# Pairs of tokens in 512-byte packets for the opening's queries and keys, with the third unit's values on all rows and several loads moved

## The chip, the cores and the metric

The kernel runs on one core of a Trainium2 chip. The metric is the device time of one execution in microseconds (us), as the median of several runs. The engines are TensorE (PE; PEld is its weight load), VectorE (DVE), ScalarE (ACT), GpSimd (POOL) and SyncE (SP), which issues most of the DMAs.

## The reference

Three stages follow one another: chunked attention with memory tokens, an MLP with a leaky ReLU, and an MLP with a rational function, all in float32.

```python
# attention: B, H, S, D = 4, 8, 768, 64; chunks of 32 queries
k_ctx = k[:, :, l_start:r_end]          # 16 tokens left, 8 right of the chunk
k_full = np.concatenate([mem_k, k_ctx], axis=2)     # 8 memory tokens ahead
v_full = np.concatenate([mem_v, v_ctx], axis=2)
scores = scale * np.matmul(q_c, k_full.transpose(0, 1, 3, 2))
a = np.exp(scores - np.max(scores, axis=-1, keepdims=True))
a = a / (np.sum(a, axis=-1, keepdims=True) + 1e-09)
out[:, :, c_start:c_end] = np.matmul(a, v_full)
# first MLP: 3072 tokens, 512 -> 2048 -> 512
h = x @ w_in;  x = np.maximum(0.01 * h, h) @ w_out
# second MLP, the same sizes
h = x @ w_in;  P = a0 + a1*h + a2*h**2 + a3*h**3
Q = 1 + abs(b0)*abs(h) + abs(b1)*h**2
out = (P / (Q + 1e-6)) @ w_out
```

The weights arrive as float64 and are read as pairs of 32-bit words.

## The kernel before, in words

The 3072 tokens are cut into six tiles of 512. Each MLP goes over its tiles, and in each over 16 columns of 128 hidden features: `emit_h` makes a column (`hps`), `leaky` or `rational` its activation, `emit_y` or `emit_o` adds its share to four accumulators (`acc`). A float32 product is made of three: each operand is split into a rounded part and a rest (`xh`, `xl`; `wh`, `wl`). A weight pair (`pair_load`, `pair_scale` on ScalarE, `pair_join` on VectorE, `pair_hi` on ScalarE, `pair_lo` on VectorE) holds one column of `w_in` and one of `w_out`, which is why the first tile of the first MLP also prepares all weights.

Attention comes in three forms. The **opening** makes the first 512 tokens before any MLP work, as four units of 128 tokens: `unit_k` and `unit_q` (transposes on TensorE, then copies into `okT` and `oqT`), `unit_b` (a copy into a ring on GpSimd), `unit_s` (scores of a unit), `unit_m` (maximum and subtraction, VectorE), `unit_e` (exponential, ScalarE), `unit_n` (sum and division), `unit_t` (transposes of the weights, copies into `pT`), `unit_x` (product with the values), `side_h` and `side_l` (split into `xh` and `xl`). Then `emit_first` makes the first columns of `hps` (L841). The **narrow** form (`att_*`) makes the second tile beside the first tile's MLP, 64 tokens at a time, and the **wide** form (`wide_*`) the others, 128 at a time, turning q and k through DRAM (`turn_out`, `turn_in` with the `park` tensors).

What sets the order: the opening is written out by hand under a manual schedule, in which each engine takes its instructions in the order of the code. In the main loop, `narrow_plan` and `wide_plan` put their steps into numbered slots, two for each column. All loads but a few are issued by SP in the order of the code. In the opening the loads of q and k are eight DMAs of 128 tokens with one token and head per packet (256 bytes), L978 and L986; then come the values (`room_v`, 16 DMAs, L320) and the weights (L167). After the opening's code come the loads of the weight pairs 2 to 4, of the narrow queries and keys, of the narrow values for blocks 8 and 9 (`load_v`, with their memory rows L344), and the coefficients (L1075, L1076). The next pair's load, the sixth, is issued in the main loop by `pairs_ahead`.

Units 0 and 1 have their weights for the product with the values on all 128 rows (two halves of 64 context rows, zero where they don't belong, written by two copies of 64 rows each); units 2 and 3 keep one copy of 128 rows and take twice as many products of 32 columns on 64 rows.

Of the kernel before, what the change touches and what calls it, by code (L numbers as in the profile page):

```python
# [16 lines left out]
P = 128  # L17
QB = 64
# [6 lines left out]
def kernel(  # L25
# [92 lines left out]
    pmore = wpool.tile([P, 2 * H * QB], F32, tag="w", name="pmore")  # L118
# [274 lines left out]
    pT = [t.rearrange("p n e c m k -> p (n e c) m k") for t in (pall, pall2)]  # L393
    pT += [pmore[:, u * H * QB:(u + 1) * H * QB] for u in range(2)]
    kraw = [early[0][:, u * H * D:(u + 1) * H * D] for u in range(U)]
    qraw = [early[1][:, u * H * D:(u + 1) * H * D] for u in range(U)]
# [15 lines left out]
    def turn(t, rows, ps):  # L412
        for c in range(NP):
            nc.tensor.transpose(ps[:, c * rows:(c + 1) * rows], t[:rows, c * P:(c + 1) * P], ident[:rows, :rows])
        return ps[:, :NP * rows].rearrange("p (c m) -> p c m", c=NP)
# [4 lines left out]
    def unit_small():  # L420
        pv = turn(sraw, NS, psa.tile([P, 512], F32, tag="acc", name="pso"))
# [4 lines left out]
        def border(u, i):  # L426
            for half in range(2):
                nc.vector.tensor_copy(out=okT[half][:, :, TAT + u * P:TAT + u * P + RCTX],
                                      in_=pv[:, half * HP:(half + 1) * HP, NM + i * RCTX:NM + (i + 1) * RCTX])

        border(1, 0)
        return lambda: border(U, 1)

    def unit_k(u, engs):
        pv = turn(kraw[u], P, psw.tile([P, 512], F32, tag="ps", name="psk"))
        at = TAT + u * P
        lo = RCTX if u == 1 else 0
        for half, eng in enumerate(engs):
            copy_on(eng, okT[half][:, :, at + lo:at + P], pv[:, half * HP:(half + 1) * HP, lo:])

    def unit_b(u, eng):
        n = P // CHUNK
        to, at = u * n % RING, RING + u * n
        for half in range(2):
            eng.tensor_copy(out=okB[half][:, :, to:to + n, NM:], in_=okB[half][:, :, at:at + n, NM:])

    def unit_q(u):
        pv = turn(qraw[u], P, psw.tile([P, 512], F32, tag="ps", name="psq"))
        nc.scalar.mul(out=oqT[:, :, u * P:(u + 1) * P], in_=pv, mul=scale)
# [3 lines left out]
    def unit_s(u):  # L453
        ps = psw.tile([P, 512], F32, tag="ps", name="pss").rearrange("p (c b m) -> p c b m", b=2, c=NP)
        for b in range(2):
            at = (2 * u + b) * QB
            for p in range(NP):
                for e in range(2):
                    r = slice(e * 64, e * 64 + 64)
                    for c in range(2):  # L460
# [4 lines left out]
                                         okB[p // HP][r, p % HP, lo:hi + 1:hi - lo, :], start=True, stop=True)  # L465
        ops[u] = ps
# [24 lines left out]
    def unit_t(u):  # L491
# [9 lines left out]
        if u >= 2:  # L501
# [5 lines left out]
    def unit_x(u):  # L507
        if u < 2:
            oxv[u] = psa.tile([P, 512], F32, tag="acc", name="psx")
# [7 lines left out]
        if u == 2:  # L517
            oxv[2] = [psw.tile([P, 512], F32, tag="ps", name="psx").rearrange("p (c u m) -> p c u m", c=NP, u=2)
                      for b in range(2)]
        pt = pT[u].rearrange("p (c e h m) -> p c e h m", c=NP, e=2, h=2)  # L520
        order = [(c, p, b) for p in range(NP) for c in range(2) for b in range(2)]
        if u == U - 1:
            order.sort(key=lambda x: (x[0], x[0] * x[2]))
        for c, p, b in order:
            r = slice(b * SB, b * SB + SB)
            for e in range(2):
# [716 lines left out]
```

## Time and profile before

| | us |
|---|---|
| median of three runs (1139.67 to 1139.99) | 1139.88 |
| the profiled execution | 1139.51 |
| its span, first to last instruction | 1137.7 |
| TensorE busy | 1127.1 |
| first `hps` matmul starts | 27.41 |

Granted TensorE clock 1.00 in all slices of the profile, full speed. All times in the rows below count from the start of the span, so a difference found in them is a difference of the execution. Busy times of TensorE overlap a little, since matmuls are pipelined; what matters is when a group starts and whether an idle time, in brackets, stands behind it.

### The profile page before, as it was taken

What the parts mean: (1) busy time and instruction counts of PE and PEld (TensorE: products, weight loads), DVE (VectorE), ACT (ScalarE), POOL (GpSimd) and SP (SyncE); (2) the same over time, 40 slices, a digit from 0 to 9 for tenths busy, and PEclk for the clock granted to TensorE, in tenths of its full rate; (3) what the DMA queues carried; (4) which work ended last, traced back from release to release, by engine and by line L of the source; (5) the groups of instructions that cost most, each with busy time, mean ns of one, the idle gap of its engine ahead of it and who ended that gap; (6) DMA issues with size and microseconds to landing.
All of it is one profiled execution on the core that took longest, in us unless ns stands there. A gap on an engine that the chain in (4) does not pass through costs nothing.

```text
span 1137.7 us, 19657 instructions
## 1 busy us (share of the span) xinstructions
PE 1127.1 (99%) x7626; PEld 922.3 (81%) x7626; DVE 766.0 (67%) x1315; ACT 628.5 (55%) x1138; POOL 237.4 (21%) x274
## 2 busy tenths in 40 slices
PE   8999999999999999999999999999999999999998
PEld 6777788888888888888888888888888888888887
DVE  5888754555645555542346886887887887788775
ACT  5687422232232223223347777776776777777765
POOL 5000302132211332210000222221222222222222
PEclk9999999999999999999999999999999999999999
DMA  9876777797778778732343002001001100100000
GB/s 208 240 223 201 192 228 209 202 257 200 209 210 237 195 203 238 215 114 94 93 138 119 21 1 74 1 1 62 13 1 37 39 1 17 58 1 3 35 1 37
DMA packets 146921, 131.59 MB, mean 116 GB/s; under 512 B 61744, under 2 KB 117392, under 8 KB 146828
## 3 DMA queue, kind: packets, MB, share of 16 engines
q1 hardware_dynamic: 141604, 122.80, 38.0%
q0 software_dynamic: 4864, 7.45, 2.8%
q8 instruction: 60, 0.98, 0.4%
q14 instruction: 33, 0.27, 0.1%
q10 hardware_dynamic: 360, 0.08, 0.0%
HBM read 92.52 MB, written 37.75 MB: 115 GB/s over the span
## 4 chain that ended last, share of the span: by engine, by line
PE 94%; SPq 2%; DMA 2%; DVE 1%; ACT 1%; issue 0%; DVEq 0%; ACTq 0%
PE hps L853 44%; PE acc L949 23%; PE acc L911 22%; PE psx L754 2%; SPq L320 1%; PE pss L712 1%; DMA wr<-in_moe_w_out_dram 1%; DMA early<-in_v_dram 0%; SPq L344 0%; SPq L167 0%; DMA early<-in_q_dram 0%; PE psx L601 0%; PE pss L554 0%; DMA pb<-park_dram 0%; PE hps L841 0%
## 5 line engine op out<-in xcount | busy, mean ns | idle before, releaser
L911 PE MATMUL acc<-g,w 128*128 128x512 f32 x1152 | 278.3, 391 | 0.0
L949 PE MATMUL acc<-w,g 128*128 128x512 f32 x1152 | 275.5, 389 | 0.0
L949 PEld LDWEIGHTS acc<-w,g 128*128 128x128 f32 x1152 | 216.3, 188 | 44.8
L911 PEld LDWEIGHTS acc<-g,w 128*128 128x128 f32 x1152 | 214.9, 188 | 45.0
L889 POOL TENSOR_TENSOR g<-R,g 128x512 fp32r<-128x512 f32 x96 | 124.4, 1296 | 504.4 <-ACT g L888 449.6
L863 ACT ACTIVATE g<-hps 128x512 fp32r<-128x512 f32 x96 | 57.4, 598 | 300.7 <-PE hps L853 300.7
L853 PE MATMUL hps<-xh,w 128*128 128x512 f32 x752 | 205.2, 396 | 0.4 <-DVE w L195 0.4
L853 PE MATMUL hps<-yh,w 128*128 128x512 f32 x768 | 204.1, 389 | 0.0
L866 DVE TENSOR_TENSOR g<-s,g 128x512 fp32r<-128x512 f32 x96 | 66.3, 690 | 179.8 <-ACT s L864 176.6
L853 PEld LDWEIGHTS hps<-yh,w 128*128 128x128 f32 x768 | 144.2, 188 | 29.9
L853 PEld LDWEIGHTS hps<-xh,w 128*128 128x128 f32 x752 | 138.5, 188 | 30.1 <-DVE w L195 0.8
L677 POOL DMA_DIRECT2D vb<-in_v_dram x128 | 83.2, 651 | 262.6 <-PE psx L754 211.5
L876 ACT ACTIVATE A<-hps 128x512 f32<-128x512 f32 x96 | 57.1, 595 | 113.9 <-PE hps L853 113.8
L892 DVE SCALAR_TENSOR_TENSOR A<-A,small,pb 128x512 f32<-128x512 f32 x96 | 72.0, 750 | 55.9 <-ACT pb L877 55.8
L853 PE MATMUL hps<-yl,w 128*128 128x512 f32 x384 | 102.7, 389 | 0.0
L853 PE MATMUL hps<-xl,w 128*128 128x512 f32 x376 | 100.9, 390 | 0.0
L883 DVE SCALAR_TENSOR_TENSOR A<-A,pb 128x512 f32<-128x512 f32 x96 | 66.8, 695 | 30.1 <-ACT pb L896 30.1
L853 PEld LDWEIGHTS hps<-yl,w 128*128 128x128 f32 x384 | 72.1, 188 | 14.9
L853 PEld LDWEIGHTS hps<-xl,w 128*128 128x128 f32 x376 | 70.6, 188 | 15.3
L878 ACT ACTIVATE R<-hps,small 128x512 f32<-128x512 f32 x96 | 75.0, 781 | 0.0
L885 DVE SCALAR_TENSOR_TENSOR R<-R,small,A 128x512 f32<-128x512 f32 x96 | 72.2, 752 | 3.4
L894 DVE SCALAR_TENSOR_TENSOR R<-R,small,hps 128x512 f32<-128x512 f32 x96 | 71.8, 748 | 3.4
(126 smaller groups left out, 1136.7 us busy)
## 6 DMA issues: line engine op xcount, KB each, us to landing
wr<-in_moe_w_in_dram SPq DMA_DIRECT2D x32, 512.0 KB
wr<-in_moe_w_out_dram SPq DMA_DIRECT2D x32, 512.0 KB
park_dram<-pb SPq DMA_DIRECT2D x16, 512.0 KB
pb<-park_dram SPq DMA_DIRECT2D x64, 128.0 KB
w_dram<-wwall SPq DMA_DIRECT2D x32, 256.0 KB
wb<-w_dram SPq DMA_DIRECT2D x32, 256.0 KB
kb<-in_k_dram SPq DMA_DIRECT2D x59, 112.0 KB
vb<-in_v_dram POOLq DMA_DIRECT2D x118, 56.0 KB, 3.5
```

Of the source, the lines that this page charges most:

```text
L677: nc.gpsimd.dma_start(out=vw[r + at:r + at + n, c], in_=v[bi, hs, lo:lo + n, :].rearrange("h p d -> p h d"))
L853: nc.tensor.matmul(ps[:, :n], w_[:, ws], x_[:, kk, :], start=(kk == 0 and m == 0), stop=(kk == KC - 1 and m == 2))
L863: nc.scalar.activation(out=gh, in_=ps, func=AF.Prelu, alpha=0.01)
L866: return [lambda: nc.vector.tensor_tensor(out=gl, in0=s, in1=gh.bitcast(F32), op=ALU.subtract)]
L878: nc.scalar.activation(out=R, in_=ps, func=AF.Identity, scale=ncf[:, 3:4], bias=ncf[:, 2:3])
L883: nc.vector.scalar_tensor_tensor(out=A0, in0=A0, scalar=ONE, in1=U0, op0=ALU.add, op1=ALU.mult)
L885: nc.vector.scalar_tensor_tensor(out=R0, in0=R0, scalar=ncf[:, 0:1], in1=A0, op0=ALU.add, op1=ALU.mult)
L889: nc.gpsimd.tensor_tensor(out=gl, in0=R0, in1=gh.bitcast(F32), op=ALU.subtract)
L892: nc.vector.scalar_tensor_tensor(out=A, in0=A, scalar=babs[:, 1:2], in1=U, op0=ALU.mult, op1=ALU.add)
L894: nc.vector.scalar_tensor_tensor(out=R, in0=R, scalar=ncf[:, 1:2], in1=ps, op0=ALU.add, op1=ALU.mult)
L911: nc.tensor.matmul(acc[i][d][:, :n], w_[:, ws], g_, start=(f == 0 and m == 0), stop=(f == FC - 1 and m == 2))
L949: nc.tensor.matmul(acc[i][s], g_[:, ss], w_, start=(f == 0 and m == 0), stop=(f == FC - 1 and m == 2))
```

## The change

1. The opening's q and k are loaded as groups of 256 tokens: partition p holds tokens 2p and 2p+1 of each head, which lie together in DRAM, so a packet has 512 bytes. The first group comes in two halves of four heads each (L995 on of the new file), the second whole: six DMAs instead of eight.
2. A transposed tile then holds the two tokens of a pair in its upper and lower 64 rows. `pairs_out` parts them by four copies of 64 rows by 256 columns for each half of the heads, with a step of two in the output. The first group's and the second queries' copies alternate between ScalarE and VectorE (`mix`); the second keys' are on ScalarE.
3. Scores and ring copies are made by halves of the heads, and the order of the units is new. Unit 2 now has its weights on all 128 rows, as units 0 and 1.
4. Unit 3's multiplication by the reciprocal sum goes from VectorE to GpSimd, and one cast of its output from ScalarE to VectorE.
5. The values of blocks 8 and 9 are loaded in the main loop, behind the weight pair of that column; the coefficients are loaded and scaled near the end of the first MLP. The first wide block's loads come three slots earlier, its queries' transposes and their reading back two.

The diff, cut to its core:

```diff
@@ views
-    pT += [pmore[:, u * H * QB:(u + 1) * H * QB] for u in range(2)]
-    kraw = [early[0][:, u * H * D:(u + 1) * H * D] for u in range(U)]
+    pT = [t.rearrange("p n e c m k -> p (n e c) m k") for t in (pall, pall2, pall)] + [pmore]
+    kraw, qraw = ([early[n][:, g * 2 * H * D:(g + 1) * 2 * H * D].rearrange("p (h m) -> p h m", h=H)
+                   for g in range(G)] for n in range(2))
@@ helpers
+    def pairs_of(src, g, hs):
+        return src[0, hs, g * 2 * P:(g + 1) * 2 * P, :].rearrange("h (p t) d -> p h (t d)", t=2)
+
+    def turn_pairs(t, half, ps):
+        for i in range(H // 2):
+            nc.tensor.transpose(ps[:, i * P:(i + 1) * P], t[:, half * (H // 2) + i], ident)
+
+    def pairs_out(ps, o, to, lo, engs, op):
+        for e in range(2):
+            for t in range(2):
+                i = ps[t * 64:t * 64 + 64].rearrange("p (c e m) -> p c e m", c=HP, e=2)[:, :, e, lo:]
+                op(engs[2 * e + t], o[e * 64:e * 64 + 64, :, to + 2 * lo + t:to + 2 * P:2], i)
...
+    def pairs_k(g, half, engs):
+        p, tag = (psa, "acc") if g else (psw, "ps")
+        ps = p.tile([P, 512], F32, tag=tag, name="psk")
+        turn_pairs(kraw[g], half, ps)
+        pairs_out(ps, okT[half], TAT + g * 2 * P, RCTX // 2 if g else 0, engs, copy_on)
...
+    def pairs_q(g, half, engs):
+        ps = psw.tile([P, 512], F32, tag="ps", name="psq")
+        turn_pairs(qraw[g], half, ps)
+        pairs_out(ps, oqT[:, half * HP:(half + 1) * HP], g * 2 * P, 0, engs, scale_on)
@@ wide_plan
-        put(at[n0] - 7, lambda: wide_load_qk(n0))
-        put(at[n0] - 6, lambda: wide_q(n0))
-        put(at[n0] - 5, lambda: turn_in(0, n0, wqT[n0]), lambda: wide_k(n0))
+        put(at[n0] - 10, lambda: wide_load_qk(n0))
+        put(at[n0] - 8, lambda: wide_q(n0))
+        put(at[n0] - 6, lambda: turn_in(0, n0, wqT[n0]))
+        put(at[n0] - 5, lambda: wide_k(n0))
@@ first loads
+        load_pairs(kraw, k, 0, LOWER)
...
+        load_pairs(qraw, q, 0, LOWER)
+        load_pairs(kraw, k, 0, UPPER)
+        load_pairs(qraw, q, 0, UPPER)
...
+        load_pairs(kraw, k, 1)
+        load_pairs(qraw, q, 1)
@@ the opening (new order)
+        mix = (act, dve, act, dve)
+        pairs_k(0, 0, mix)
+        unit_small()
+        unit_b(0, 0, pool)
+        unit_b(1, 0, pool)
+        pairs_q(0, 0, mix)
+        pairs_k(0, 1, mix)
...
+        unit_s(0, 0)
+        unit_s(1, 0)
+        pairs_q(0, 1, mix)
+        unit_s(0, 1)
+        unit_s(1, 1)
+        unit_m(0)
+        unit_m(1)
...
+        pairs_k(1, 0, (act,) * 4)
+        unit_e(0)
+        pairs_k(1, 1, (act,) * 4)
+        unit_e(1)
+        unit_n(0, pool)
+        pairs_q(1, 0, mix)
+        pairs_q(1, 1, mix)
...
+        unit_s(3, 1)
+        unit_m(2)
+        spread = unit_t(0)
+        unit_m(3)
+        run(spread)
+        unit_e(2)
...
+        unit_x(2)
...
+        side_h(2)
+        side_l(1)
+        unit_x(3)
+        warm(3)
+        side_h(3, 0)
+        side_h(3, 1, dve)
         emit_first(0, (0, 2))
-        load_v(FIRST)
-        load_v(FIRST + 1)
-        nc.sync.dma_start(out=coef[:, 0:4], in_=a.partition_broadcast(P))
-        nc.sync.dma_start(out=coef[:, 4:6], in_=b.partition_broadcast(P))
@@ main loop
-                if c == FC:
+                if c == NA - FC + 2:
+                    nc.sync.dma_start(out=coef[:, 0:4], in_=a.partition_broadcast(P))
+                    nc.sync.dma_start(out=coef[:, 4:6], in_=b.partition_broadcast(P))
+                if c == NA - 5:
                     nc.scalar.mul(out=ncf, in_=coef[:, 0:4], mul=-1.0)
...
                 pairs_ahead()
+                if c < 3:
+                    load_v(FIRST + c - 1)
```

The order of instructions at three places follows. On **ScalarE, in the opening**, around the four exponentials (`psk` and `psq` are transposed keys and queries, `pm` the scores on their way to weights, `pst` transposed weights, `psx` products). Before:

```order
L480 ACTIVATE pm<-pm 128x512
L418 COPY early<-psk 128x2x128 x2
L449 ACTIVATE early<-psq 128x4x128
L418 COPY early<-psk 128x2x128 x2
L449 ACTIVATE early<-psq 128x4x128
L480 ACTIVATE pm_104<-pm_104 128x512
L499 COPY pb<-pst 64x16x32 x2
L480 ACTIVATE pm_104<-pm_104 128x512
L538 CAST xh<-psx 128x4x128
L480 ACTIVATE pm_105<-pm_105 128x512
```

Now:

```order
L428 COPY early<-psk 64x2x124 x4
L496 ACTIVATE pm<-pm 128x512
L428 COPY early<-psk 64x2x124 x4
L496 ACTIVATE pm_104<-pm_104 128x512
L452 ACTIVATE early<-psq 64x2x128 x4
L515 COPY pb<-pst 64x16x32 x2
L496 ACTIVATE pm_104<-pm_104 128x512
L515 COPY pb_106<-pst 64x16x32 x2
L496 ACTIVATE pm_105<-pm_105 128x512
```

The second group's copies stand between the exponentials, and the fourth exponential stands behind the copies of unit 1's weights.

On **SP, behind the opening**, from the fourth weight pair's load to the sixth's (`wr` are weights, `vb` narrow values, `kb` and `qr` narrow keys and queries, `small` the coefficients). Before:

```order
L167 DMA wr_99<-in_moe_w_out_dram 128x1024
L320 DMA kb<-in_k_dram 96x8x64
L344 DMA vb<-in_mem_v_dram 8x8x64 x2
L320 DMA vb<-in_v_dram 56x8x64 x2
L344 DMA vb<-in_mem_v_dram 8x8x64 x2
L320 DMA vb<-in_v_dram 56x8x64 x2
L1075 DMA small<-in_moe_a_dram 128x4
L1076 DMA small<-in_moe_b_dram 128x2
L167 DMA wr_100<-in_moe_w_in_dram 128x4x256
```

Now:

```order
L167 DMA wr_99<-in_moe_w_out_dram 128x1024
L320 DMA kb<-in_k_dram 96x8x64
L167 DMA wr_100<-in_moe_w_in_dram 128x4x256
L167 DMA wr_100<-in_moe_w_out_dram 128x1024
L344 DMA vb<-in_mem_v_dram 8x8x64 x2
L320 DMA vb<-in_v_dram 56x8x64 x2
L325 DMA qr<-in_q_dram 128x8x64
```

The sixth pair's load (`wr_100`) stands directly behind the keys; eight loads of values and two of coefficients are gone from in front of it.

On **VectorE, beside the first tile's last columns**, around the first wide block's transposes (`qT` queries, `pb` keys; L195 is `pair_lo`). Before:

```order
L181 SCALAR_TENSOR_TENSOR wwall<-wr_605,wwall 128x1024
L686 STREAM_TRANSPOSE qT<-qr 128x4x2x32 x2
L611 TENSOR_TENSOR xl<-psx,xh 128x4x64
L866 TENSOR_TENSOR g<-s,g 128x512
L695 STREAM_TRANSPOSE pb<-kb 128x4x2x32 x4
L195 TENSOR_TENSOR w<-wwall,w 128x2x512
```

Now:

```order
L181 SCALAR_TENSOR_TENSOR wwall<-wr_598,wwall 128x1024
L626 TENSOR_TENSOR xl<-psx,xh 128x4x64
L882 TENSOR_TENSOR g<-s,g 128x512
L710 STREAM_TRANSPOSE pb<-kb 128x4x2x32 x4
L195 TENSOR_TENSOR w<-wwall,w 128x2x512
```

The queries' two transposes left this place; they stand one column earlier, behind the join of the pair before.

## Rows read from the trace of the kernel before

**Rows 1.** The page: busy us, share of the span and instructions of each engine.

```profile
PE 1127.1 (99%) x7626; PEld 922.3 (81%) x7626; DVE 766.0 (67%) x1315; ACT 628.5 (55%) x1138; POOL 237.4 (21%) x274
```

**Rows 2.** Waits of TensorE over the whole span: us in total, times, longest.

```profile
PE pss L554 <- ACT kT L379: 1.2, 1, 1.2
PE pss L712 <- DMA pb<-park_dram: 0.8, 1, 0.8
...
PE hps L853 <- DVE w L195: 0.4, 1, 0.4
```

**Rows 3.** TensorE in order of time, opening: start us, us, what [idle before].

```profile
4.08 1.06 PE L414 MATMUL psk<-ident,early 128*128 128x128 f32 x4
...
12.01 0.63 PE L414 MATMUL psk<-ident,early 128*128 128x128 f32 x4 [0.58 <-DMA early<-in_k_dram]
...
14.29 1.10 PE L464 MATMUL pss<-early 64*32 64x64 f32 x64
15.32 0.66 PE L495 MATMUL pst<-ident,pm 128*128 128x128 f32 x4
...
23.72 2.95 PE L527 MATMUL psx<-pmore,early 64*64 64x32 f32 x128
...
27.41 2.11 PE L841 MATMUL hps<-xh,w 128*128 128x512 f32 x8
...
30.68 2.21 PE L841 MATMUL hps<-xh,w 128*128 128x512 f32 x8 [0.26 <-ACT w L189]
```

**Rows 4.** DMA packets and rates: 2 to 13, 28 to 33, 181.5 to 182.

```profile
DMA packets 9296, 2.35 MB, mean 214 GB/s; under 512 B 9295, under 2 KB 9295, under 8 KB 9295
...
DMA packets 1165, 1.83 MB, mean 366 GB/s; under 512 B 51, under 2 KB 945, under 8 KB 1164
...
DMA packets 154, 0.08 MB, mean 152 GB/s; under 512 B 6, under 2 KB 154, under 8 KB 154
```

**Rows 5.** ScalarE in order of time, opening.

```profile
10.94 0.63 ACT L418 COPY early<-psk 128x256 f32<-128x256 f32 x2
11.47 0.60 ACT L449 ACTIVATE early<-psq 128x512 f32<-128x512 f32 x1
...
16.08 1.17 ACT L499 COPY pb<-pst 64x512 f32<-64x512 f32 x2 [0.26 <-PE pst L495]
```

**Rows 6.** VectorE in order of time, opening.

```profile
6.87 0.49 DVE L424 COPY early<-pso 128x128 f32<-128x128 f32 x2 [5.34 <-PE pso L414]
...
15.46 0.69 DVE L475 TENSOR_REDUCE mx<-pss 128x8 f32<-128x512 f32 x1 [0.31 <-PE pss L464]
...
16.79 0.67 DVE L486 TENSOR_REDUCE sm<-pm 128x8 f32<-128x512 f32 x1
...
17.83 0.64 DVE L475 TENSOR_REDUCE mx<-pss 128x8 f32<-128x512 f32 x1
...
28.11 0.42 DVE L178 TENSOR_SCALAR wwall<-wwall 128x512 uint32<-128x512 uint32 x1
```

**Rows 7.** GpSimd in order of time, opening.

```profile
18.08 1.04 POOL L489 TENSOR_TENSOR pm<-pm,sm 128x512 f32<-128x512 f32 x1 [0.90 <-DVE sm L488]
```

**Rows 8.** ScalarE in order of time, 44 to 58 us.

```profile
53.67 1.13 ACT L171 ACTIVATE wwall<-wr 128x1024 f32<-128x1024 f32 x1 [1.60 <-DMA wr<-in_moe_w_out_dram]
```

**Rows 9.** The chain that ended last, in order of time: start us, us, what.

```profile
25.58 1.09 PE psx L527 x31
...
46.74 6.82 DMA wr<-in_moe_w_out_dram
```

**Rows 10.** VectorE, SP and TensorE in order of time, 119 to 142 us.

```profile
120.46 0.70 DVE L178 TENSOR_SCALAR wwall<-wwall 128x1024 uint32<-128x1024 uint32 x1 [0.92 <-ACT wwall L171]
...
123.59 0.77 DVE L686 STREAM_TRANSPOSE qT<-qr 128x256 f32<-128x256 f32 x2
...
126.52 1.76 SPq L640 DMA_DIRECT2D qT<-park_dram  x4
...
135.69 0.78 PE L712 MATMUL pss<-pb,qT 64*32 64x64 f32 x56 [0.85 <-DMA pb<-park_dram]
```

More of the change, by code (lines that the diff above doesn't have):

```diff
@@ L410, in tokens, with load_pairs @@
         return src[0, :, lo:lo + n, :].rearrange("h p d -> p h d")
[L412 to L415, printed above, removed]
+    def pairs_of(src, g, hs):
+        return src[0, hs, g * 2 * P:(g + 1) * 2 * P, :].rearrange("h (p t) d -> p h (t d)", t=2)
+    def load_pairs(raws, src, g, hs=slice(0, H)):
+        nc.sync.dma_start(out=raws[g][:, hs], in_=pairs_of(src, g, hs))
+    def turn_pairs(t, half, ps):
[6 more added lines that the diff above has]
+                op(engs[2 * e + t], o[e * 64:e * 64 + 64, :, to + 2 * lo + t:to + 2 * P:2], i)
     def copy_on(eng, out, in_):
@@ L420, in unit_small @@
     def unit_small():
-        pv = turn(sraw, NS, psa.tile([P, 512], F32, tag="acc", name="pso"))
+        ps = psa.tile([P, 512], F32, tag="acc", name="pso")
+        for c in range(NP):
+            nc.tensor.transpose(ps[:, c * NS:(c + 1) * NS], sraw[:NS, c * P:(c + 1) * P], ident[:NS, :NS])
+        pv = ps[:, :NP * NS].rearrange("p (c m) -> p c m", c=NP)
         for half in range(2):
@@ L425, in unit_small @@
                                   in_=i[:, :, 0:NM].unsqueeze(2).to_broadcast([P, HP, RING, NM]))
[L426 to L439, printed above, removed]
@@ L447, in unit_q, with unit_s @@
-    def unit_q(u):
-        pv = turn(qraw[u], P, psw.tile([P, 512], F32, tag="ps", name="psq"))
-        nc.scalar.mul(out=oqT[:, :, u * P:(u + 1) * P], in_=pv, mul=scale)
+        eng.tensor_copy(out=okB[half][:, :, to:to + n, NM:], in_=okB[half][:, :, at:at + n, NM:])
     ops = {}
-    def unit_s(u):
-        ps = psw.tile([P, 512], F32, tag="ps", name="pss").rearrange("p (c b m) -> p c b m", b=2, c=NP)
+    def unit_s(u, half):
+        if u not in ops:
+            ops[u] = psw.tile([P, 512], F32, tag="ps", name="pss").rearrange("p (c b m) -> p c b m", b=2, c=NP)
+        ps = ops[u]
@@ L455, in unit_s @@
         for b in range(2):
             at = (2 * u + b) * QB
-            for p in range(NP):
+            for p in range(half * HP, (half + 1) * HP):
                 for e in range(2):
@@ L507, in unit_x @@
     def unit_x(u):
-        if u < 2:
-            oxv[u] = psa.tile([P, 512], F32, tag="acc", name="psx")
+        if u < U - 1:
+            pool_, tag = (psw, "ps") if u == 2 else (psa, "acc")
+            oxv[u] = pool_.tile([P, 512], F32, tag=tag, name="psx")
             xv = oxv[u].rearrange("p (c b h m) -> p c b h m", c=NP, b=2, h=2)
```

130 lines of the change are left out of this document (55 added, 75 removed).

## The prediction

> **What bounds the kernel now.** I read the page first, then TensorE's waits, then the opening in order of time. The page shows TensorE busy for 1127.1 us, 99% of the span of 1137.7 us [rows 1], so only 10.6 us are to be won by better feeding; everything else must come from TensorE's own work. The table of TensorE's waits shows where idle time after the opening lies: 1.2 us once before `pss` L554, 0.8 us once before `pss` L712 and 0.4 us once before `hps` L853, 2.4 us in all [rows 2]. The rest is the opening, the 27.41 us before the first matmul of the first MLP tile (L841), with the second column of that MLP at 30.68 us [rows 3]. From there TensorE has no gap until the 1.2 us wait. So the change is worth two things: by how much it moves the start of the second `hps` column, and which of the three later waits it removes. The profiled execution took 1139.51 us, 0.37 us less than the median of 1139.88; I make differences against the profile and apply them to the median.
>
> **The loads of the opening.** Eight DMAs of 256 KB become four of 256 KB and two of 512 KB, in packets of 512 bytes instead of 256. Between 2 and 13 us all packets were 256 bytes and moved 214 GB/s; weight packets of 1 and 4 KB moved 366 GB/s between 28 and 33 us; the only stretch with almost nothing but 512-byte packets, the later keys on 28 partitions, moved 152 GB/s [rows 4]. No row shows 512-byte packets on 128 partitions, so 152 and 366 are the ends. I take 290, the middle of 214 and 366, because these tiles fill all partitions as the 256-byte tiles and the weights do. The first tile was transposed from 4.08 us [rows 3]; I keep that, with its bytes through at 3.25 us. From there the seventh tile's bytes (six more of 0.262 MB at 214 GB/s) were through at 10.6 us, and it was waited for until 12.01 [rows 3]: landing lags by 1.4 us. At 290 GB/s (0.9 us a tile) this gives: first queries, lower heads, 5.5 us; keys, upper heads, 6.5; queries, upper heads, 7.4; second keys 9.2; second queries 11.0. All loads behind them start about 2 us earlier.
>
> The Trainium skill, page "DMA: Bandwidth & Descriptors", section "Why small descriptors are slow (HBM only)", speaks against a large gain: 3 extra beats for each descriptor, so 8 of 11 beats carry data at 256 bytes and 16 of 19 at 512. By that rule 512-byte packets would move 214 x (16/19) / (8/11) = 248 GB/s, an estimate from that page; the opening would then end 0.25 us later than my sum below, and the result would be 1138.5 us. The trace leaves room for both: 366 GB/s is above what the rule's ratio gives from 214, 152 below.
>
> **The chain of the opening.** Here the cost lies. Prices: 32 score matmuls 1.03 us from start to next start (14.29 to 15.32), four transposes 0.66 or 0.58 in a row [rows 3]; on ScalarE a copy of 256 columns 0.27 and an operation of 512 columns 0.5 in the queue (two copies from 10.94 to 11.47), two 64-row copies of 512 columns 1.15, with 0.1 more until a result is used [rows 5]; on VectorE the two maximum operations 1.33 and the three of the sum 1.04 (15.46, 16.79, 17.83), a copy of 128 columns 0.2, so 0.34 for 256 [rows 6]; on GpSimd the multiplication 1.04 [rows 7]. A copy of 64 rows costs as much as one of 128: the split by parity and head doubles the copies of q and k, from 8 of k (256 columns) and 4 of q (512) to 32 of 256, on ScalarE and VectorE.
>
> (1) First transposes 4.1 to 4.8, four copies (two on each engine) to 5.6, VectorE's four small copies to 6.3, first queries' copies 6.3 to 7.05, scores of the lower heads of units 0 and 1 7.1 to 8.15, transposes of the upper queries to 8.8, their copies to 9.6, scores of the upper heads of unit 0 to 10.25. The first maximum starts at 10.3 us.
>
> (2) TensorE then does unit 1's half and the second keys (to 11.4). ScalarE goes through four key copies from 11.45 (1.1), the first exponential (0.5), four key copies (1.1), the second exponential (0.5), four query copies (1.1): the last ends at 15.95. VectorE is full as well: a memset, two maxima, one sum, four query copies, one sum, 6.6 us from 10.3, to 17.0. The scores of units 2 and 3 end at 17.6, four halves of 0.52 behind the queries, and only then does the transpose of unit 0's weights follow (18.2), because it now stands behind both. Two copies (19.4), third exponential, two copies, fourth exponential (21.7), sum (22.9), multiplication on GpSimd instead of VectorE's 0.69 (24.0), transpose (24.7), then TensorE's third unit (1.1, on all rows) and at 25.75 the fourth. Half of the 2.95 us of 128 records at L527 [rows 3] is 1.48: 27.2. The last casts, side by side on ScalarE and VectorE, end at 27.7. First `hps` at 27.8, **0.35 us later** than before. The third unit gains 0.35 us by its full rows and no longer stands behind the last transpose, but the chain ahead is longer.
>
> (3) The second `hps` column hangs on VectorE: now a cast (0.34), one subtraction of 512 columns (0.61), two of 256 (0.34 each) before the weights' join. From the join's start to the second column it was 30.68 - 28.11 = 2.57 us [rows 3, 6]; so 27.3 + 1.65 + 2.55 = 31.5 against 30.68. **The opening costs 0.85 us.** Rates above 290 GB/s don't help, since TensorE's order and the copies then set every step; at 214 GB/s the upper keys land at 7.1 and the opening costs 1.4, at 152 GB/s the second queries land at 16.8 and it costs 4.2. These are its bounds from loads; to the other side, every landing could be early without more than 0.1 us of gain.
>
> **The later waits.** (a) At 55.2 us TensorE waits 1.21 us for a copy on ScalarE behind the scaling L171, which waited 1.60 us for weights [rows 8]. In the chain these were issued at 46.7 us and landed 6.82 us later [rows 9]; the order of SP shows eight value loads and two of coefficients ahead of them. Now those weights come before the values, which are read first at L601, behind this wait on TensorE, and the coefficients go to the end of the first layer. ScalarE would do the scaling at once, 0.4 us ahead of need: minus 1.21. What comes late next is the queries' tile, which waits for its reader; nothing on TensorE waits for that until the weights of a later pair, issued no later than now. (b) The transposes of the first wide queries, 0.77 us on VectorE at 123.59, stand one column earlier, ahead of one more of the waits of 0.92 us that VectorE has for ScalarE there [rows 10]. The weights' subtraction behind them comes 0.7 us earlier and the wait of 0.40 us goes. (c) On SP the four reads of the queries, 1.76 us from 126.52, stood between the keys' transposes and their write; they now come before, and the transposes are 0.7 us earlier, so the last read of the keys lands 2.4 us earlier. Wanted are 0.85 us [rows 10] and 0.8 us by which TensorE comes earlier: minus 0.85. The coefficients' two scalings, of 4 and 2 columns on ScalarE, move with their loads off every path here: nothing. The loads of the wide keys wait for a reader that is done by then. Sum of (a) to (c): 2.46.
>
> **Sum:** 0.85 - 2.46 = -1.6 us: 1137.9 against the profile, **1138.3** against the median, 0.14% less. A measurement of this kernel tells about 0.2% (2.28 us) from no change.
>
> **Rivals.** *The loads set the opening.* For it: in the chain the last value tile landed just ahead of 25.58, and only then did the fourth unit go on [rows 9]. With 2.2 us saved on queries and keys and SP free earlier it would land near 22. If that were the whole limit, `hps` would start at 24.0 and the time be 1134.0; if half, 1135.7, which is its price. Against it: 31 of the 128 records of units 2 and 3 were left then [rows 9], so the chain of exponentials ended almost together with the load. Chance 0.18. *The later waits stay,* or turn up in the next column since VectorE has no slack there: with (a) alone left, 1139.5. Chance 0.18. *Slower, by late queries.* The two 512 KB loads stand behind one another, and TensorE's scores of units 2 and 3, with unit 0's transposes behind them, wait for the second queries. From a landing after 13 us on, each us goes into the opening; from 15 us on (about 178 GB/s) the change loses more than (a) to (c) give. At 152 GB/s: 4.2 - 2.46 = +1.7, 1141.6. For it: the only row with 512-byte packets. Against it: 28 partitions there, 128 here. Chance 0.08.
>
> **How the numbers follow.** My forecast has 0.56, with its own range 1137.2 to 1139.4 (a step of the chain wrong by 0.5 us, 214 GB/s, a remainder of a wait). The range 1136.2 to 1140.8 leaves out about half of the first rival and the slow one. Faster by over 0.2% is below 1137.6: most of the first rival (0.16) and the low quarter of mine (0.14), 0.30; slower, above 1142.2, a part of the last, 0.04; the same, 0.66.
>
> **What would show it.** Right: the first maximum on VectorE at 10 to 11 us, ScalarE without a gap from 11.5 to 16, first `hps` at 27.5 to 28.5, the second 3.7 us behind, none of the three waits in TensorE's table. Wrong: first `hps` before 27 us (loads were the limit), second queries waited for after 13 us, or a wait over 0.5 us between 50 and 60 us.

## The result, and the profile after

The changed kernel takes 1148.29 us, median of 6 runs (1148.05 to 1149.31), where 6 runs of the kernel before on the same chip have a median of 1140.13. The ratio is 1.0059, 95% interval 1.0044 to 1.0074: **slower by 0.6%**, where 0.14% less was forecast. The profiled execution took 1148.24 us with a span of 1146.5.

The three later waits are gone, and all that was lost was lost in the opening. TensorE's line of the page, and its waits over the whole span (us in total, times, longest), answer to [rows 1, 2]:

```profile
PE 1132.1 (99%) x7592; PEld 926.3 (81%) x7592; DVE 771.0 (67%) x1326; ACT 632.1 (55%) x1147; POOL 239.4 (21%) x275
...
PE pss L481 <- DVE early L454: 6.0, 7, 1.8
...
PE psx L531 <- issue: 1.1, 1, 1.1
PE hps L857 <- ACT w L189: 0.6, 1, 0.6
```

Neither `kT`, nor `park_dram`, nor the later column of `hps` is in that table any more (the 0.6 us before `hps` L857 stand in the opening). In the opening, scores wait seven times for query copies (`early` L454). TensorE is busy for 5.0 us more with 34 instructions fewer: some of its work ran slower.

TensorE in order of time, the opening (start us, us, what, [idle before]), answers to [rows 3]:

```profile
4.09 1.06 PE L419 MATMUL psk<-ident,early 128*128 128x128 f32 x4
5.92 1.11 PE L419 MATMUL psq<-ident,early 128*128 128x128 f32 x4
...
9.71 0.43 PE L481 MATMUL pss<-early 64*32 64x64 f32 x4 [1.82 <-DVE early L454]
10.50 1.92 PE L481 MATMUL pss<-early 64*32 64x64 f32 x60 [0.36 <-DVE early L454]
12.35 1.12 PE L419 MATMUL psq<-ident,early 128*128 128x128 f32 x4
14.50 0.43 PE L481 MATMUL pss<-early 64*32 64x64 f32 x4 [1.03 <-DVE early L454]
...
38.77 2.08 PE L857 MATMUL hps<-xh,w 128*128 128x512 f32 x8
42.37 2.21 PE L857 MATMUL hps<-xh,w 128*128 128x512 f32 x8 [0.60 <-ACT w L189]
```

The first `hps` starts at 38.77 us instead of 27.41, the second column at 42.37 instead of 30.68: the opening costs 11.69 us. Less the 2.46 us of the three waits that is 9.2; the spans differ by 8.8.

ScalarE and VectorE in order of time around the first tile answer to [rows 5, 6] (a name with q behind it is the engine's queue, here issuing loads):

```profile
5.02 1.48 ACTq L1003 DMA_DIRECT2D early<-in_mem_v_dram  x2
6.60 0.38 ACT L428 COPY early<-psk 64x256 f32<-64x256 f32 x1 [4.57 <-DMA early<-in_k_dram]
7.47 0.38 ACT L428 COPY early<-psk 64x256 f32<-64x256 f32 x1 [0.49 <-DVE early L428]
...
18.34 1.57 ACT L428 COPY early<-psk 64x248 f32<-64x248 f32 x4 [3.57 <-PE psk L419]
19.94 0.63 ACT L496 ACTIVATE pm<-pm 128x512 f32<-128x512 f32 x1
...
7.01 0.43 DVE L428 COPY early<-psk 64x256 f32<-64x256 f32 x1 [5.49 <-ACT early L428]
7.88 0.43 DVE L428 COPY early<-psk 64x256 f32<-64x256 f32 x1 [0.44 <-ACT early L428]
...
16.79 0.69 DVE L491 TENSOR_REDUCE mx<-pss 128x8 f32<-128x512 f32 x1
```

The four copies of one tile do not run two and two: they run ScalarE 6.60, VectorE 7.01, ScalarE 7.47, VectorE 7.88, each waiting for the one before on the other engine. The idle time in brackets is the other engine's copy; the change from one engine to the other takes about 0.03 us (6.98 to 7.01). A tile takes 1.7 us (6.60 to 8.31) in place of 0.8. And the first copy starts at 6.60, though its tile was transposed by 5.15, because ScalarE's queue was still issuing the two loads of the memory's values.

TensorE's groups by shape from 5 to 20 us (busy us, mean ns), after and then before:

```profile
L481 PE MATMUL pss<-early 64*32 64x64 f32 x128 | 4.7, 311 | 3.6 <-DVE early L454 3.6
L419 PE MATMUL psq<-ident,early 128*128 128x128 f32 x14 | 3.7, 429 | 0.0
```
```profile
L464 PE MATMUL pss<-early 64*32 64x64 f32 x256 | 4.4, 218 | 0.0
L414 PE MATMUL psq<-ident,early 128*128 128x128 f32 x16 | 2.5, 280 | 1.3 <-DMA early<-in_q_dram 1.3
```

The same scores take 311 ns each instead of 218 and transposes 429 instead of 280. So there are three suspects beside the order of the units: the alternating copies, TensorE's rate, and ScalarE's queue. The loads are none: from 3 to 9 us they ran as forecast (290 GB/s):

```profile
DMA packets 3569, 1.75 MB, mean 292 GB/s; under 512 B 207, under 2 KB 3569, under 8 KB 3569
```

### The profile page after: what moved, and what is told of

It is laid out like the page before. It is cut to its first block, busy times and chain, and to the rows that moved or that the text cites. A ratio compares the mean times of both kernels' runs of the same rounds, so it can differ in the third digit from the quotient of the medians.

```text
span 1146.5 us, 19616 instructions
## 1 busy us (share of the span) xinstructions
PE 1132.1 (99%) x7592; PEld 926.3 (81%) x7592; DVE 771.0 (67%) x1326; ACT 632.1 (55%) x1147; POOL 239.4 (21%) x275
## 4 chain that ended last, share of the span: by engine, by line
PE 97%; ACT 1%; DVE 1%; DMA 0%; issue 0%; SPq 0%; ACTq 0%; DVEq 0%
PE hps L869 46%; PE acc L927 23%; PE acc L965 23%; PE psx L769 2%; PE pss L727 1%; PE pss L481 0%; PE psx L616 0%; PE pss L569 0%; DMA early<-in_k_dram 0%; PE psx L531 0%; DVE early L454 0%; ACT early L428 0%; PE psk L377 0%; PE hps L857 0%; ACT early L452 0%
```

## The experiments

Marks of an opening come from one profiled execution each, and the same opening has its first `hps` at 27.41 and at 28.48 us in two kernels: differences under about 1 us mean little by themselves. Executions of the kernel before spread from 1138 to 1147 us, so the ratios, each against runs of the kernel before on the same chip, carry the times.

The third maximum is that of the third unit. In the changed kernel it comes 11.6 us late, so the whole loss lies ahead of it. Behind it, in all runs but e8 and the kernel before, TensorE stands idle for 0.3 to 2.9 us under "issue", an idle time that the profile gives no cause for. Up to the first `hps` it has only two places, behind 343 to 345 and behind 467 to 470 records of matmuls, whatever the opening does; its length differs from run to run. It delays the first `hps` and can hide a gain there. What it is stays open.

| run | first maximum | third maximum | first `hps` | median us | ratio (95%) |
|---|---|---|---|---|---|
| before | 8.95 | 15.46 | 27.41 | 1140.13 | 1 |
| changed | 16.79 | 27.09 | 38.77 | 1148.29 | 1.0059 (1.0044 to 1.0074) |
| e1 loads alone | 9.15 | 15.55 | 28.48 | 1138.70 | 0.9982 (0.9967 to 0.9997) |
| e2 opening alone | 16.76 | 27.03 | 40.16 | 1151.01 | 1.0081 (1.0055 to 1.0108) |
| e3 two banks | 14.62 | 22.85 | 36.43 | 1145.93 | 1.0031 (1.0014 to 1.0048) |
| e10 apart outputs | 15.66 | 25.71 | 38.04 | 1147.25 | 1.0060 (1.0042 to 1.0078) |
| e17 one bank, e3's division | 16.34 | 26.12 | 39.02 | 1148.39 | 1.0057 (1.0040 to 1.0074) |
| e7 one engine a tile | 16.85 | 26.35 | 41.22 | 1148.61 | 1.0072 (1.0057 to 1.0088) |
| e4 pauses filled | 14.96 | 24.36 | 38.32 | 1148.39 | 1.0059 (1.0036 to 1.0082) |
| e5 memory's values moved | 15.14 | 25.43 | 39.19 | 1147.76 | 1.0061 (1.0040 to 1.0082) |
| e12 e3 and e4 | 14.15 | 21.61 | 33.83 | 1143.31 | 1.0028 (1.0013 to 1.0043) |
| e6 e3, e4 and e5 | 11.76 | 19.24 | 32.01 | 1143.80 | 1.0027 (1.0014 to 1.0040) |
| e15 TensorE's order alone | 14.67 | 24.95 | 37.77 | 1147.24 | 1.0053 (1.0032 to 1.0073) |
| e14 e6 and order | 12.34 | 19.96 | 32.01 | 1141.23 | 1.0001 (0.9988 to 1.0014) |
| e16 e14, keys ahead | 11.79 | 18.61 | 30.58 | 1141.33 | 1.0000 (0.9986 to 1.0014) |
| e11 e6, half the copies | 12.07 | 18.23 | 30.80 | 1140.46 | 0.9995 (0.9981 to 1.0009) |
| e8 loads and values | 9.00 | 15.54 | 28.36 | 1138.95 | 0.9990 (0.9978 to 1.0003) |
| e13 e8, sides earlier | 11.09 | 15.96 | 29.09 | 1138.10 | 0.9988 (0.9973 to 1.0003) |

### The change in two halves (e1, e2)

e1 is the kernel before with the diff's last part alone; e2 is the changed kernel without it.

```diff
-        load_v(FIRST)
-        load_v(FIRST + 1)
-        nc.sync.dma_start(out=coef[:, 0:4], in_=a.partition_broadcast(P))
...
+                if c < 3:
+                    load_v(FIRST + c - 1)
```

> The kernel before with only the moved loads (the values of the first two blocks behind the first two passes, the coefficients behind them, the wide loads up to three steps earlier). Theory (the moved loads take away the three later waits and do nothing else): 2.46 us less than the kernel before, about 1137.5, and no wait of TensorE above 0.3 us after 45 us. Rival (these waits went only because the longer opening of the changed kernel gave the transfers more time): no change, with the 1.21 us wait near 55 us still there.

> The changed kernel with the loads put back where they stood, so the new opening alone. Theory (opening and loads add up): first hps at 38.8 and about 11 us over the kernel before, 1151; if the later start of the accumulation also uses up the 1.21 us wait near 55 us, 1149.5 to 1150. Rival (the moved loads themselves slow the opening): first hps back near 28 and the time within 1 us of the kernel before.

e1 is faster than the kernel before, by 0.18% (0.03 to 0.33%), about 2.1 us, and so beats both kernels. Its table of TensorE's waits has lost the waits (a) and (b), 1.61 us, but (c) stayed:

```profile
PE pss L712 <- DMA pb<-park_dram: 1.0, 1, 1.0
```

The 1.61 us lie within the interval of that gain. In e2, the new opening with the old loads, (a) is gone too, by the later start alone, while (b) and (c) stand:

```profile
PE pss L727 <- DMA pb<-park_dram: 1.2, 2, 0.7
...
PE hps L868 <- DVE w L195: 0.4, 1, 0.4
```

So (c) went with neither half alone, only with both, and why is not shown: in e14 below, which has the moved loads and an earlier start than the changed kernel, it is back with 0.8 us, and in nine other runs 0.2 to 0.9 us of "issue" stand at its place. The rival of e1, that the waits went only because the longer opening gave the transfers more time, holds for none of them: (a) and (b) went in e1 without it, and (b) and (c) stand in e2 with it. e2 is 2.7 us above the changed kernel by the medians, 2.5 by the ratios, whose intervals overlap: with the new opening the loads are worth about as much as without it. The loss is the opening's alone.

### Why the copies stand one behind the other (e3, e10, e17, e7)

e3 transposes the two heads of a pair into two PSUM tiles; ScalarE then reads only the one, VectorE only the other.

```diff
-            nc.tensor.transpose(ps[:, i * P:(i + 1) * P], t[:, half * (H // 2) + i], ident)
+            nc.tensor.transpose(ps[i % 2][:, i // 2 * P:(i // 2 + 1) * P], t[:, half * (H // 2) + i], ident)
...
-        mix = (act, dve, act, dve)
+        mix = (act, act, dve, dve)
```

> The changed kernel with the two heads of a pair of columns transposed into two PSUM tiles, one read by ScalarE alone and one by VectorE alone. Theory (the four copies of a tile stand one behind the other because both engines read one bank): the waits of one engine for the other within a tile are gone, a tile's copies take 0.8 to 0.9 us in place of 1.73, the first maximum starts 2 to 4 us earlier than at 16.8 and the first hps comes 3 to 6 us earlier than at 38.8. Rival (the loads or TensorE's slow opening set the time): copies side by side, but first maximum and first hps within 1 us of the changed kernel's.

ScalarE and VectorE in order of time, the same first tiles in e3:

```profile
6.73 0.77 ACT L428 COPY early<-psk 64x256 f32<-64x256 f32 x2 [4.71 <-DMA early<-in_k_dram]
7.52 0.82 ACT L452 ACTIVATE early<-psq 64x256 f32<-64x256 f32 x2
...
5.19 0.86 DVE L428 COPY early<-psk 64x256 f32<-64x256 f32 x2 [3.66 <-PE psk L419]
```

No copy waits for the other engine; VectorE is through its half before ScalarE, held by its queue, begins. The first maximum comes 2.2 us earlier, at the lower edge of what the theory gave, the third 4.2. The first `hps` comes 2.3 us earlier, less than the 3 to 6 of the theory, behind 2.3 us of "issue" (1.1 in the changed kernel).

e10 keeps one bank and writes the parities to separate columns. e17 keeps one bank and takes e3's division of the copies.

```diff
-                op(engs[2 * e + t], o[e * 64:e * 64 + 64, :, to + 2 * lo + t:to + 2 * P:2], i)
+                at, n = to + 2 * lo, P - lo
+                op(engs[2 * e + t], o[e * 64:e * 64 + 64, :, at + t * n:at + t * n + n], i)
```

> The changed kernel, but the two parities are written to two separate runs of columns and not between one another, so that no two copies of a tile write near each other (the tokens then stand in another order than the scores take them for: the output is of permuted keys and queries). Theory (what orders the two engines is the bank that both read): copies still alternate, 1.73 us a tile, first hps within 0.5 us of 38.8. Rival (they are ordered, or slowed, because their outputs lie between one another): copies of ScalarE and VectorE side by side, first hps 2 to 5 us earlier.

> The changed kernel with one PSUM tile for both heads, as it is, but ScalarE copying both parities of the one head and VectorE those of the other, the division of the run with two banks. Theory (the bank orders the engines): still one wait of an engine for the other in each tile and two copies behind two, 1.6 to 1.75 us a tile, first maximum within 0.6 us of 16.8, so not the 14.6 that two banks gave. Rival (the division of the copies did it, not the bank): copies side by side and the first maximum at 14.6, as with two banks.

VectorE in e10, and then in e17:

```profile
6.95 0.43 DVE L429 COPY early<-psk 64x256 f32<-64x256 f32 x1 [5.42 <-ACT early L429]
7.80 0.43 DVE L429 COPY early<-psk 64x256 f32<-64x256 f32 x1 [0.43 <-ACT early L429]
```
```profile
7.53 0.86 DVE L428 COPY early<-psk 64x256 f32<-64x256 f32 x2 [6.00 <-ACT early L428]
...
16.34 0.69 DVE L491 TENSOR_REDUCE mx<-pss 128x8 f32<-128x512 f32 x1
```

With outputs apart the waits of 0.43 and 0.49 us stay (the first `hps` is 0.7 us earlier, a little more than the 0.5 that the theory allowed); with e3's division, but one bank, VectorE's two stand behind ScalarE's two. Together with e3 this shows it: what orders the two engines is the one PSUM tile, a bank, that both read. The Trainium skill, page "PSUM — Partial Sum Buffer", section "PSUM bank collisions raise a hardware error", asks to guard PSUM by bank and quadrant of partitions, and calls guarding by bank alone the simple version. In the changed kernel ScalarE read rows 0 to 63 and VectorE rows 64 to 127 of the tile, so by that rule they need not have been ordered; the traces show that they were. No run here took the order away inside one bank, or put two tiles into one, so whether the program's order goes by the tile or by the bank stays open.

e7 gives every tile of keys to ScalarE and every tile of queries to VectorE.

```diff
-        pairs_k(0, 0, mix)
+        pairs_k(0, 0, (act,) * 4)
...
-        pairs_q(0, 0, mix)
+        pairs_q(0, 0, (dve,) * 4)
```

> The changed kernel with one bank for a tile as it is, but all four copies of a tile of keys on ScalarE and all four of a tile of queries on VectorE, so that no bank is read by both. Theory (the cost is the order of two engines on one bank): no wait of one engine for the other within a tile, a tile 1.55 to 1.75 us as now, but a tile of keys and one of queries side by side, so first maximum and first hps 1 to 3 us earlier than 16.8 and 38.8. Rival (the copies cost by their number on either engine, the sharing nothing): within 0.5 us of the changed kernel.

A miss: nothing is gained, and the first maximum stays where the rival had it (the first `hps` is 2.4 us later, with 2.9 us of "issue" ahead of it). Within a tile nothing waits any more, but four copies in a row on one engine took 1.56 and 1.75 us, as long as four that alternate. The first keys had nothing beside them, since VectorE's border copies stand ahead of its query copies and wait for ScalarE's keys until 8.06 us. The first queries and the next keys did go side by side (8.66 and 8.63 us), but the next queries were transposed only behind the first scores, at 12.39 us as in the changed kernel (12.35). Avoiding the bank is worth something where it shortens a tile's copies, as in e3.

### TensorE's rate (e4)

```diff
+        heat(5)
         unit_s(0, 0)
...
+        heat(3)
         unit_s(0, 1)
```

> The changed kernel with five products without use ahead of the first scores and three ahead of the second half's, where TensorE waited 1.8 and 1.0 us. Theory (the pauses keep TensorE at the lower of its two rates): transposes fall from 421 ns to about 273 before 13 us and the score products from 304 to about 216, and the first hps comes 1 to 3 us earlier. Rival (TensorE's rate is a matter of time since the start, or the copies alone set the opening): still 421 and 304 ns there, first hps unchanged or up to 0.5 us later.

TensorE in e4, and then in e5 (below), where the pause was left:

```profile
10.39 1.08 PE L481 MATMUL pss<-early 64*32 64x64 f32 x60 [0.33 <-DVE early L454]
11.41 0.66 PE L419 MATMUL psq<-ident,early 128*128 128x128 f32 x4
```
```profile
5.76 0.66 PE L419 MATMUL psq<-ident,early 128*128 128x128 f32 x4
8.07 0.43 PE L481 MATMUL pss<-early 64*32 64x64 f32 x4 [1.00 <-DVE early L454]
8.86 1.92 PE L481 MATMUL pss<-early 64*32 64x64 f32 x60 [0.36 <-DVE early L454]
10.71 1.11 PE L419 MATMUL psq<-ident,early 128*128 128x128 f32 x4
```

TensorE's busy time, granted clock, DMA share and GB/s in e5:

```profile
6.00:8.00 2.00, 1.07 (x8) 0.98 1.18 304
8.00:10.00 2.00, 1.57 (x48) 0.50 1.19 273
```

Filled, 60 scores take 1.08 us and four transposes 0.66, as in the kernel before. In e5 TensorE was at that rate at 5.76 us, stood idle for 1.00 us, and then took 1.92 and 1.11, with a granted clock of 0.50 (1.2 GHz): the rate fell at the pause. So it is not a matter of time since the start. The changed kernel's first query transposes, at 5.92 us, already took 1.11 us, before any copy had made TensorE wait: there it had not risen yet. So the waiting copies are only part of why its rate was low. Filling brought the first maximum 1.8 us earlier and the third 2.7. Of that, 2.0 us were left at the start of the last group of products (34.96 us for 36.97) and 0.45 at the first `hps`; in e4, but not in the changed kernel, TensorE stood idle within that group:

```profile
36.98 0.71 PE L542 MATMUL psx<-pmore,early 64*64 64x32 f32 x33 [1.36 <-issue]
```

The time did not move.

### ScalarE's queue (e5), and all three (e12, e6)

```diff
-            nc.scalar.dma_start(out=vroom[U - 1][b_ * SB:b_ * SB + NM, 1], in_=mem_v[0].rearrange("h p d -> p h d"))
...
         load_pairs(qraw, q, 1)
+            nc.sync.dma_start(out=vroom[U - 1][b_ * SB:b_ * SB + NM, 1], in_=mem_v[0].rearrange("h p d -> p h d"))
```

> The changed kernel with the two loads of the memory's values moved from ScalarE's queue to the end of the opening's loads on SyncE's queue, so that ScalarE's first copy has no load ahead of it. Theory (these loads wait for earlier ones and hold ScalarE until 6.6 us, which delays the whole chain): the first copy of keys starts at about 5.2 in place of 6.6, first maximum and first hps come 1.0 to 1.5 us earlier, time 1147. Rival (the alternating copies have slack there, or the memory's values come late on the other queue): first hps within 0.4 us of 38.8 or later.

The first copy of keys starts at 4.96 us, the first maximum 1.65 us earlier, a little more than expected, and the third 1.7; the first `hps` not at all (39.19), with 1.64 us of "issue" in the last group of products.

> Two banks and the products without use, with the memory's values left on ScalarE's queue. Theory (ScalarE's late first copies matter once banks and rate are mended): first maximum 1.2 to 1.6 us later than with all three edits (11.8), first hps 1.0 to 1.6 us later than 32.0. Rival (the place of these loads is worth nothing, as it was alone): first hps within 0.4 us of 32.0.

> The changed kernel with all three edits: two PSUM tiles for a pair's two heads, products without use in TensorE's two long pauses, and the memory's values on SyncE's queue. Theory (bank order, TensorE's rate and the queue each delay the first maximum, and add up): first maximum near 11 to 12 in place of 16.8, first hps at 31 to 34, time 1140 to 1143. Rival (the units' order, with both units' scores ahead of the first maximum and eight copies of ScalarE ahead of its exponentials, sets the opening): first hps stays above 35.

Together the three are worth 7.85 us of the third maximum (27.09 to 19.24), where each alone gave 4.2, 2.7 and 1.7: on this mark they nearly add up, as the theory had it. At the first `hps` they are worth 6.8 us (38.77 to 32.01), more than the sum of each alone (2.3, 0.45, nothing): between the two marks each single gain lost about 2 us and the joint one 1.1, and "issue" has a part in that. e12 against e6 says that the queue is worth 1.8 us of first `hps` once the others are mended, a little more than expected, but the times don't show it (ratios 1.0028 and 1.0027). The median of e6, 1143.80 us, lies above the 1140 to 1143 of its theory and gained less than its marks. The profiled execution does not show why, since it is one of the fastest (1141.34) and its span is 6.9 us under the changed kernel's. In it the first column ran at the lower rate for a while, and the second came 4.42 us behind the first, against 3.60 in the changed kernel. Windows of e6 (us, then busy time of each engine, granted clock, DMA share, GB/s), and TensorE's row:

```profile
22.00:32.00 10.00, 7.56 (x172) 5.69 (x173) 6.46 (x13) 7.37 (x14) 4.46 (x6) 1.00 1.06 355
32.00:36.00 4.00, 4.00 (x12) 3.20 (x12) 3.90 (x9) 1.93 (x4) 0.00 (x0) 0.58 1.19 247
...
32.01 3.66 PE L857 MATMUL hps<-xh,w 128*128 128x512 f32 x8
```

A granted clock of 0.58 is mostly the level of 1.2 GHz, and eight matmuls took 3.66 us where the changed kernel's took 2.08. TensorE was idle for 2.4 of the 10 us before. But in e14, below, it was idle for as long there and kept a clock of 1.00, so what made the rate fall is not shown.

### What was left (e15, e14, e16, e11)

e15 puts the second half's query transposes ahead of the first scores in the changed kernel; e14 does that to e6 (with three products to fill) and loads the memory's values earlier; e16 also moves half the second pair's keys ahead of the first maximum; e11 is e6 without the odd tokens' copies of the second pair.

```diff
         pairs_k(0, 1, mix)
+        pairs_q(0, 1, mix)
...
-        pairs_q(0, 1, mix)
+        pairs_k(1, 0, (act,) * 4)
         unit_s(0, 1)
```

> The changed kernel with nothing but the second half's query transposes ahead of the first scores. Theory (the order of TensorE's queue adds its part beside the shared bank): VectorE's and ScalarE's copies of these queries start at about 12 in place of 13.5 and first maximum and first hps come 1 to 1.5 us earlier than 16.8 and 38.8. Rival (the alternating copies of earlier tiles are the whole wait): less than 0.4 us.

> The kernel with all three edits, the second half's query transposes put ahead of the first scores (three products without use behind them in place of five and three), and the memory's values loaded ahead of the last loads of the first 256 tokens and not behind all of them. Theory (TensorE's order holds the second query copies back: they waited 1.5 us behind scores that themselves waited): first maximum at 10.3 to 11 in place of 11.8, POOL's copies of the memory's values done by 13.5 in place of 14.9, first hps 1 to 2 us earlier than 32.0. Rival (ScalarE and VectorE are full and hand the gain back): first maximum earlier, first hps within 0.5 us of 32.0.

> As the first of these three, and the first half of the second 256 keys transposed and copied ahead of the first maximum, where ScalarE waited (10.4 to 12.3 with all three edits). Theory (what is left is ScalarE's queue: eight key copies between the two first exponentials): third maximum 1.0 to 1.6 us earlier than in the first of the three, first hps 0.8 to 1.6 us earlier. Rival (POOL's border copies and products, or VectorE's query copies, are the last): less than 0.4 us.

> The kernel with all three edits, but the copies of the odd tokens of the second 256 tokens left out, for keys and queries (their places are set to zero ahead of the opening, so those rows of the output are not the reference's). Of the eight copies of keys ScalarE loses four, and of the eight copies of queries each engine two. Theory (what is left of the longer opening, 4 to 5 us, is the work of sixteen copies of 64 rows where the kernel before has six to eight wide ones): the third unit's maximum and the first hps come 1.5 to 2.5 us earlier than with all three edits (19.2 and 32.0). Rival (POOL's copies, the loads of the memory's values or the order of the units set it): less than 0.7 us earlier.

The order of TensorE's queue alone is worth 2.1 us of first and third maximum, more than its theory had, and 1.0 of first `hps`, no more than openings differ by themselves. In e14 the first maximum is not earlier but 0.6 us later (the three products ran at the lower rate, 1.49 us) and the first `hps` is at 32.01 as before: a miss, although its median is 2.6 us below e6's, for which these marks give no reason. e16 brings the third maximum from 19.96 to 18.61 and the first `hps` from 32.01 to 30.58, as ScalarE's queue theory said, but its median stays. Leaving out eight copies gives 1.0 us of third maximum and 1.2 of first `hps`, between theory and rival. So of the 11.4 us by which the first `hps` was late, 8.2 are accounted for by bank, rate, queue and order (38.77 to 30.58); the third maximum gives the same (8.5 of 11.6). The copies' number has a part in the other 3.2, and the rest of them is not settled. Repaired as far as e16, the changed kernel is where the kernel before is, with the moved loads, worth 2.1 us alone, included.

### The third unit's values, and a better version (e8, e13)

e8 is e1 with the third unit's values on all rows; e13 takes its low halves earlier.

```diff
         side_h(1)
+        side_l(0)
         run(unit_t(3))
...
+        side_l(1)
         side_h(2)
```

> The kernel before with the moved loads and the third unit's values on all rows (its products 32 in place of 64, the fourth unit's copies split). Theory (the third unit's products stand on the path ahead of first hps): 0.5 to 1.5 us less than with the moved loads alone, 1136.5 to 1138 where the kernel before has 1140.6. Rival (the two more copies of 64 rows and the block of zeros that has to be reused cost what the products save): within 0.3 us of the moved loads alone.

> The kernel before with moved loads and third unit's values on all rows, and the low halves of the first two units' results taken before the weights of the first column's second part. Theory (the second hps column waited 1.2 us for ScalarE's weight copy because eight result copies came in one row): second column at 31 to 31.8 in place of 33.2, time 0.5 to 1.5 us under the moved loads with the values alone. Rival (the weights' own chain on VectorE is late by that work wherever it stands): second column still after 32.5 and no difference.

In e8 the first `hps` was at 28.36, and TensorE had now to wait 0.9 us for value tiles ahead of it; the second column came at 33.16, after 1.24 us for ScalarE's weight copy. In e13 that wait is 0.64 and the second column is 3.61 us behind the first in place of 4.80, but at 32.70, after 32.5 as its rival had it: TensorE was still at its lower rate at the first 64 scores (1.93 us, in e8 1.10). Both ratios are within the interval of e1: the third unit's rows are worth nothing that these runs can tell. e1 is the version that is faster than both kernels.

## Why the prediction was wrong, point by point

- **The opening, +0.85.** This is the term that failed: it cost 11.69 us. Its steps (1) and (2) follow below, with what they were priced by.
- **Later waits, -2.46.** Right in the changed kernel: all three are gone. Alone, the moved loads are worth about 2.1 us; (c) is not theirs alone, and (a) would have gone with the later start.
- **Loads, 290 GB/s.** Right: 292. The Trainium skill's estimate from page "DMA: Bandwidth & Descriptors", section "Why small descriptors are slow (HBM only)", 248 GB/s, was too low here. The rival of late queries had no part in the loss.
- **Step (1), "four copies (two on each engine) to 5.6".** Here it failed first, and with the largest single part: two banks alone win back 4.2 of the 11.6 us at the third maximum. I took the engines to work side by side; the program orders them by the tile, a bank, that both read. The lateness against my chain grows along it: the first tile's copies end at 8.31 for 5.6, and the first maximum starts at 16.79 for 10.3. Of the first 2.7 us the alternation has 0.9; the first copy starts 1.8 late, of which e5 won back 1.64 by the queue. A misreading stands there too: [rows 3] has the first transposes at 1.06 us, and they took that again, to 5.15 and not to 4.8.
- **The same step, what stands ahead on ScalarE.** I listed the queue of SP and took ScalarE to be free at 4.8. Its two loads of the memory's values were issued from 5.02 to 6.50, where e1, with the old loads, has them at 2.07.
- **"32 score matmuls 1.03", "four transposes 0.66".** The prices were those of TensorE at its higher rate. At the lower one, which it had in this opening, they were 1.92 for 60 and 1.11.
- **"A copy of 256 columns 0.27".** On ScalarE four in a row took 1.57, so 0.39 each, on VectorE 0.43 for 0.34. In the kernel before, the second of two copies of 128 rows begins 0.27 behind the first, before that has ended; copies of 64 rows stood one behind the other's end. [rows 5] had it: two 64-row copies of 512 columns at 1.17 us, against 0.5 in the queue for an operation of 128 rows. So "a copy of 64 rows costs as much as one of 128" does not hold in ScalarE's queue.
- **Step (2), ScalarE full from 11.45 to 15.95.** The form was right (18.34 to 25.44, nearly without a gap until the queries' alternation), the start 6.9 us late, the length 2.6 us more.
- **The rival on the slow side** was late loads, at 1141.6. A cost in the copies stood in no rival: I bounded the rate of the loads from both sides, and the copies, a new kind of work for two engines on one tile, from none.

## What to carry to other kernels

Before work on one PSUM tile is given to two engines, count it as serial, and give each engine a bank of its own if it is to be parallel. Price such a chain as the sum of both engines' steps (four copies took 1.71 us here, of which the changes of engine were about 0.03 each), and with TensorE at its lower rate at the start and wherever the chain makes it pause. When a gain is made of two independent parts, measure the parts: here the small one was worth 2.1 us and the large one lost 11. And compare chains at a mark ahead of idle times that nobody changed.

## What was not expected of the hardware

In the opening of the changed kernel TensorE's records show a lower rate from the first transposes on (60 scores in 1.92 us for 1.08), and yet the granted clock reads 1.00 in every window there (us, TensorE's busy time, granted clock, DMA share, GB/s):

```profile
10.00:12.00 2.00, 1.64 (x61) 1.00 1.18 166
```

In e5, where TensorE had risen to its higher rate at 5.76 us and fell again, the row reads 0.50 for the same work, and in e6, behind the opening, 0.58. In the kernel before, the first transposes took 1.06 us and later ones 0.63 [rows 3], again with 1.00 throughout. So here the row showed falls that came after a rise, and not the lower rate at the start, which is to be read from the records' durations. And a mended link of a chain can show nothing at the end: e4 and e5 gained 1.8 and 1.65 us at the first maximum, 2.7 and 1.7 at the third, and nothing in time, with 1.4 and 1.6 us of "issue" standing in the last group of products.
